# Splitting the first casts, deferring three row picks, and swapping a half quarter with the third convolution

## The chip, the cores and the metric

The kernel runs on one core of a Trainium2 chip. Its engines appear in the profile as PE (TensorE: matrix multiplications, with the weight loads as PEld), DVE (VectorE), ACT (ScalarE), POOL (GpSimd) and SP (SyncE, which here only issues transfers). Each engine takes its instructions in the order of the program and waits where an operand, a buffer or a transfer is not ready. The metric is the device time of one execution in microseconds (us); less is better.

## The reference

For each of 8 batches, 4096 positions and 8 heads the reference makes seven weights by a softmax, and forms a causal convolution of `x` with them (24 channels to a head). The result, 32768 rows of 192 numbers, goes through a feed-forward layer with a squared ReLU:

```python
w = np.exp(weight_gen - max);  w = w / (sum + 1e-09)          # (8, 4096, 8, 7)
out = np.einsum('bshk,bskhg->bshg', w, x_unf)                 # x_unf: 7 shifted rows of x
h = np.maximum(out.reshape(B * S, D) @ w_in, 0.0)             # 192 -> 2048
return h * h @ w_out                                          # 2048 -> 192
```

Inputs and outputs are 32-bit floats.

## The kernel before, in words

The rows are cut into 64 sub-blocks of 512. Blocks 0 and 1 hold one sub-block each, all later ones hold two. For each block there are five kinds of work:

- **Softmax** (class `Softmax`): exponentials on ACT (L238, called "E" in the plans), then sums, reciprocals and products on DVE (L245, L252, L260, called "S"). The weights end in a tile with 8 rows to a partition, `v_first`.
- **Rows and bands.** A band matrix needs the weights with one row to a partition. For the first two sub-blocks PE does this re-ordering: `select_rows` (L359) multiplies with a 0/1 matrix, 8 multiplications for each of five row tiles ("row picks"), and ACT copies each result to `wr` (L377). For later ones, DMAs do it (`wr_load_sbuf`, L351). `st_band` (L381, called "B") then spreads `wr` over a mask on DVE, and gives `bd`.
- **Convolution** ("C"): `bd` against `x` on PE (L447 for the first two sub-blocks, L519 for the next blocks), into PSUM tiles `yp`, which ACT or DVE copies to `y` (L459, L460, L462, L530).
- **Units** ("u"): `st_unit` multiplies `y` with a slice of `w_in` into a PSUM tile `h` (L549 in blocks 0 and 1, where there are 8 units, L564 after, where there are 16). ACT takes the ReLU, `t` (L578), and for each pair of units DVE squares it, `g` (L582).
- **Half quarters** ("M"): `st_mm2` multiplies `g` with `w_out` on PE into the banks o0 and o1 (L613). Every second one ends with `o_sum`: an ACT copy (L627), and from block 2 on a DVE addition (L629), before the store.

PSUM holds o0 and o1 and a ring of three larger tiles, tag "h", which picks, `yp` and `h` share: a unit can start only when the tile of three allocations before has been read.

The order is written out by hand: the program is traced in the order in which each engine is to work. What comes before the first unit is a straight list (L667 to L718). The list `plans` (L725) then has a string for each of blocks 0 to 3; steps "M" take half quarters, block after block, from one generator. In blocks 0 and 1 the four half quarters of a block are those of quarter 0 and 1 over units 0 to 3, then of quarter 0 and 1 over units 4 to 7. So of the four M in `plans[1]` three belong to block 0 and the fourth is the first of block 1.

In the straight list, `x_cast` (L333) casts all five row tiles of the first `x` from 32 to 16 bits in one ACT instruction (L335), before the picks. `st_conv_first` (L431) calls `next_rows` (L702) after each of its five tiles: one row pick of the second sub-block each time, ACT copies for the first two, and after the second the cast of the first half of `w_in` (L708, 1536 columns, on ACT). The copies of the other three rows follow the convolution.

Of the kernel before, what the change touches and what calls it, by code (L numbers as in the profile page):

```python
# [9 lines left out]
def kernel(  # L10
# [26 lines left out]
    nc = tc.nc  # L37
    f32 = mybir.dt.float32
    f16 = mybir.dt.float16

    B, S, D = x.shape
# [9 lines left out]
    P = 128  # L51
# [14 lines left out]
    NT = 5  # L66
# [4 lines left out]
    ROW_ORDER = (0, 1, 2, 3, 4)  # L71
# [9 lines left out]
    p_x = ctx.enter_context(tc.tile_pool(name="p_x", bufs=2))  # L81
# [12 lines left out]
    NQ = Dff // WQ  # L94
    w_i = const.tile([P, WQ, 2, NQ + NQ // 2], f16, name="w_i")
# [32 lines left out]
    x_st = {}  # L128
# [10 lines left out]
    def cross_w_in(q):  # L139
        for r0, r1 in ((0, RT), (RT, 0)):  # L140
            nc.sync.dma_start(out=w_i[r0 : r0 + RT, q, 1], in_=w_i[r1 : r1 + RT, q, 0])
# [147 lines left out]
    x_t, wr_t, pr_t, bd_t, yp_t, y_t, g_t, gp_t, t1_t, o_t, o_sb_t = ({} for _ in range(11))  # L289
# [12 lines left out]
    def tile_start(j, i):  # L302

        t1 = (j % NBB + 1) * TB
        return TB - P if i == NT - 1 and t1 in ends(j // NBB) else starts[i]
# [17 lines left out]
    def x_load(j):  # L323
        x_t[j] = p_x.tile([P, NT, D], f16, name="xt")
        block_load(j, x_t[j], x[j // NBB], D, nc.gpsimd)
# [4 lines left out]
            j, x_st[j][:, 0 : NT * D].rearrange("p (t d) -> p t d", t=NT), x[j // NBB], D, nc.sync  # L330
        )

    def x_cast(j, copy):  # L333
        x_t[j] = p_x.tile([P, NT, D], f16, name="xt")
        copy(out=x_t[j].rearrange("p t d -> p (t d)"), in_=x_st[j][:, 0 : NT * D])  # L335

    def wr_load(j):
        wr_t[j] = p_wr.tile([P, NT, HP, SL * 2], f16, name="wr")
# [20 lines left out]
    def select_rows(j, s, tiles, places):  # L359

        if j not in wr_t:
            wr_t[j] = p_wr.tile([P, NT, HP, SL * 2], f16, name="wr")
        for i, (pool, tag) in zip(tiles, places):
            pr = pool.tile([P, H * SL], f32, name="pr", tag=tag)
            a = max(j % NBB * TB + tile_start(j, i), 0) - s.t0
            for r in range(s.r):
                c = a + FIRST - 1 - r
                nc.tensor.matmul(  # L368
                    out=pr, lhsT=sel[:, c : c + P],
                    rhs=s.v[:, HALO + r].rearrange("p g c e -> p (g c e)"),  # L370
                    start=(r == 0), stop=(r == s.r - 1),
                )
            pr_t[(j, i)] = pr

    def copy_rows(j, tiles):
        for i in tiles:
            nc.scalar.copy(  # L377
                out=wr_t[j][:, i].rearrange("p g c -> p (g c)"), in_=pr_t.pop((j, i))
            )

    def st_band(j, tiles):  # L381


        if j not in bd_t:
            bd_t[j] = p_bd.tile([P, H * NT * STEP], f16, name="bd")
        i = tiles[0]
        lo = STEP * i
        shift = 0 if i == 0 and j % NBB == 0 else lo - tile_start(j, i)
        n = min(STEP, P - shift)
        shape = (P, HP * len(tiles), n // SL, 2 * SL)  # L390
        nc.vector.tensor_tensor(  # L391
            out=bd_t[j][:, H * lo : H * (lo + len(tiles) * n)].rearrange(
                "p (g m c) -> p g m c", g=shape[1], c=2 * SL
            ),
            in0=wr_t[j][:, i : tiles[-1] + 1]
            .rearrange("p t g c -> p (t g) c")
            .unsqueeze(2)
            .broadcast_to(shape),
            in1=mask[:, shift : shift + n]
            .rearrange("p (m c) e -> p m (c e)", c=SL)  # L400
            .unsqueeze(1)
            .broadcast_to(shape),
            op=AluOp.mult,
        )
# [26 lines left out]
    def st_conv_first(j, between=None):  # L431

        s = BLOCKS[j][0]
        y = p_y.tile([P, NK, TB], f16, name="y")
        y_t[j] = y
        yp = ps_h.tile([P, 2, TB], f32, name="yp", tag="h")
        places = [(q, 32 * q, 0) for q in range(4)]
        places += [(q, r0 + 32 * (q - 4), 1) for r0 in (0, RT) for q in (4, 5)]
        for i in ROW_ORDER:
            lo, b = bounds[i], bounds[i + 1]  # L440
            hi = lo + (STEP if tile_start(s, i) == starts[i] else b - lo)
            bd = bd_t[s][:, H * lo : H * hi].rearrange("p (g c e) -> p g e c", g=HP, e=2)
            for later in (True, False):
                for q, p0, k in places:
                    _, ha, hb, pre = quads[q]
                    m, h = (32, hb) if later else (pre, ha)
                    nc.tensor.matmul(  # L447
                        out=yp[p0 : p0 + m, k, lo:b],
                        lhsT=x_t[s][:, i, 32 * q : 32 * q + m],
                        rhs=bd[:, h // 2, h % 2, 0 : b - lo],  # L450
                        start=True,
                        stop=True,
                        skip_group_check=True,
                        tile_position=(0, p0),
                    )
            if between:
                between(i)
        if j == 0:
            nc.scalar.copy(out=y[:, 0], in_=yp[:, 0])  # L459
            nc.vector.tensor_copy(out=y[:, 1], in_=yp[:, 1])  # L460
        else:
            nc.scalar.copy(out=y[:, 0:2], in_=yp)  # L462
# [178 lines left out]
    def st_bands(j):  # L641
        first = int(j % NBB == 0)
        last = NT - int(tile_start(j, NT - 1) != starts[-1])
        for tiles in (range(first), range(first, last), range(last, NT)):
            if tiles:
                st_band(j, tiles)

    with nc.allow_low_precision("fp16 matmul pipeline"), tc.manual_schedule():
# [31 lines left out]
        s0, s1, s2 = parts[:3]  # L680
# [4 lines left out]
        w_st = p_wg.tile([P, (R + HALO) * HK], f32, name="w_st", tag="wg")[:, 0 : NQ + NQ // 2]  # L685
# [6 lines left out]
        s0.total(0, s0.rh)  # L692
        s0.recip(0, s0.rh)
        s0.scale(0, s0.rh, nc.vector)
        x_cast(0, nc.scalar.copy)
        o0, o1, ring = (ps_o, "o0"), (ps_o, "o1"), (ps_h, "h")
        select_rows(0, s0, ROW_ORDER, (o1, ring, ring, ring, o0))
        copy_rows(0, ROW_ORDER)
        for i in ROW_ORDER:
            st_band(0, (i,))  # L700

        def next_rows(i):  # L702
            n = ROW_ORDER.index(i)
            select_rows(1, s0, (i,), ((o1, ring, ring, o0, o1)[n],))
            if n < 2:
                copy_rows(1, (i,))
            if n == 1:
                nc.scalar.copy(out=w_i[:, 0, 0], in_=w_st)  # L708

        st_conv_first(0, next_rows)  # L710
        copy_rows(1, ROW_ORDER[2:])

        nc.gpsimd.tensor_copy(out=gate, in_=w_st[:, 0:1])
        for q in range(4):
# [8 lines left out]
        steady = "MuMuuu" * 3 + "MuuuMCu"  # L723
        steady_spread = "MuMuuu" * 2 + "MuCMuuu" + "MuMuuu"
        plans = {  # L725
            0: "B1 u u u u E1 C S1 u u M u u",
            1: "L3 u u B2 M E2 B3 u M E2 u u S2 S2 u M u C u M",
            2: "L4 u u u E3 M u u u M B4 u u u u M B5 S3 u u u u M u E3 C u",
            3: "L5 L6 S3 u u u M u u u M u M B6 E4 u u u M u M B7 u u u E4 M u M C S4 u",
        }  # L730

# [50 lines left out]
        for j in range(len(plans), NBLK):  # L782
            plan, u = [], 0
# [9 lines left out]
        def load_rows(j):  # L793

            s = [p for p in parts if p.fb <= j][-1]
            if s.r == FIRST:
                return
            if s in stored:
                for n in range(BLOCKS[j][0], sum(BLOCKS[j])):
                    wr_load(n)  # L800
            else:
                waiting.append((s, j))
# [40 lines left out]
        for j in range(NBLK):  # L843
            if j + 2 < NBLK:
                load_rows(j + 2)
            if j == 1:
                for q in range(WQ):
                    cross_w_in(q)
            u = 0
            for step in plans[j].split():  # L850
                kind, n = step[0], int(step[1:] or 0)
                if kind == "u":
                    st_unit(j, u)
                    u += 1
                elif kind == "M":
                    next(mm2)
                elif kind == "C" and j + 1 < NBLK:
                    st_conv(j + 1)
                    if j == 0:
                        x_load(3)  # L860
                    elif j + 2 < NBLK:
                        for k in range(BLOCKS[j + 2][0], sum(BLOCKS[j + 2])):
                            x_load(k)
                    if j == 5:
                        load_w_spread()
                    elif j == 6:
                        cross_w_spread()
                elif kind == "E":
                    parts[n].exp(*next(parts[n].exps))
                elif kind == "S":  # L870
                    soft(parts[n])
                elif kind == "B":
                    st_bands(n)
                elif kind == "L":
                    parts[n].load(nc.sync)


        j = NBLK - 1
# [44 lines left out]
```

The softmax here doesn't subtract the row's maximum and nothing guards it: scores larger than these inputs give would overflow.

## Time and profile before

| what | value |
|---|---|
| runs | 732.98 us, median of 5 (732.74 to 733.24) |
| the profiled execution | 732.74 us, span from first to last instruction 731.0 us |
| PE busy in the span | 724.5 us, 99% |
| DVE busy | 625.8 us, 86% |
| ACT busy | 612.7 us, 84% |
| POOL busy | 99.9 us, 14% |
| granted TensorE clock | 1.00 |

By stage, from the busy time of each engine in stretches of the span (us):

| stretch | what it holds | length | PE | DVE | ACT |
|---|---|---|---|---|---|
| 0 to 13.5 | up to the first unit | 13.5 | 10.84 | 8.26 | 6.70 |
| 13.5 to 22.2 | block 0 | 8.7 | 8.56 | 7.84 | 7.84 |
| 22.2 to 35.7 | block 1 | 13.5 | 13.47 | 12.23 | 12.49 |
| 35.7 to 59.7 | block 2, start of block 3 | 24.0 | 23.67 | 22.50 | 22.63 |
| 59.7 to 731.0 | the rest | 671.3 | 667.91 | 574.98 | 563.08 |

The profile is one execution on the chip. A line of the timeline has start, duration, engine, source line, operation, the tiles written and read, and how often; what stands in brackets is the idle time of the engine just before, and what ended it. A chain of waits is followed back from the last instruction, at each step to what released it. A merged line's duration runs from its first start to its last end. Ends of multiplications are modelled, so the distance between two starts says more of PE than a duration does.

### The profile page before, as it was taken

How to read it: one execution, taken by the hardware profiler on the slowest of the kernel's cores; microseconds unless marked ns; L12 is line 12 of the kernel's file. 1: busy time of each engine (PE TensorE's matmuls, PEld its weight loads, DVE VectorE, ACT ScalarE, POOL GpSimd, SP SyncE). 2: the span in 40 equal slices, each digit the busy share in tenths (PEclk: the TensorE clock that was granted, in tenths of full speed). 3: DMA queues.
4: the chain of work that ended last, by engine and by line, in shares of the span. 5: the costliest groups of instructions: out<-in, count | busy, mean ns of one | idle time of the engine just before them, and what ended most of it. 6: DMA issues, size and time to landing. Idle time of an engine off the chain costs nothing.

```text
span 731.0 us, 30985 instructions
## 1 busy us (share of the span) xinstructions
PE 724.5 (99%) x14053; PEld 529.1 (72%) x14053; DVE 625.8 (86%) x834; ACT 612.7 (84%) x731; POOL 99.9 (14%) x145
## 2 busy tenths in 40 slices
PE   8999999999999999999999999999999999999998
PEld 4658788777777777777777777777777777777777
DVE  6998998998898988888988888988889988778753
ACT  5899888888888888888888888888888888888883
POOL 8231223321001100011000010010000110001000
PEclk9999999999999999999999999999999999999999
DMA  9555445684445452455432554334544325444012
GB/s 205 114 111 109 82 78 112 142 150 121 94 66 137 87 95 56 85 117 119 72 69 63 128 113 87 56 74 119 103 88 86 57 51 119 66 87 78 30 45 68
DMA packets 125984, 68.30 MB, mean 93 GB/s; under 512 B 85321, under 2 KB 122140, under 8 KB 125340
## 3 DMA queue, kind: packets, MB, share of 16 engines
q1 hardware_dynamic: 79516, 46.79, 22.5%
q0 software_dynamic: 46192, 19.43, 22.5%
q8 instruction: 110, 1.80, 1.0%
q14 instruction: 22, 0.18, 0.1%
q10 hardware_dynamic: 144, 0.10, 0.0%
HBM read 50.18 MB, written 28.70 MB: 108 GB/s over the span
## 4 chain that ended last, share of the span: by engine, by line
PE 95%; DVE 3%; ACT 1%; DMA 0%; issue 0%; DVEq 0%
PE o L613 46%; PE h L564 42%; PE yp L485 4%; PE h L549 2%; PE yp L519 1%; DVE g L582 1%; DVE bd L391 1%; DMA wg<-in_weight_gen_dram 0%; DVE v_first L260 0%; ACT t L578 0%; DVE ssum L245 0%; DVE rcp L252 0%; PE yp L447 0%; ACT w_i L708 0%; PE pr L368 0%
## 5 line engine op out<-in xcount | busy, mean ns | idle before, releaser
L578 ACT ACTIVATE t<-h 128x1024 f16<-128x1024 f32 x512 | 496.5, 1027 | 60.7 <-PE h L564 59.2
L613 PEld LDWEIGHTS <-g 64*128 64x128 f16 (+1 forms) x8032 | 344.6, 94 | 55.1 <-issue 2.6
L613 PE MATMUL o<-w_o,g 64*128 64x192 f16 (+1 forms) x8032 | 380.5, 243 | 0.4 <-issue 0.2
L582 DVE TENSOR_TENSOR g<-t 128x2048 f16<-128x2048 f16 (+1 forms) x287 | 307.2, 1104 | 28.4 <-ACT t L578 28.1
L564 PE MATMUL h<-y,w_p 64*128 64x512 f16 x2400 | 291.7, 376 | 0.0
L564 PEld LDWEIGHTS <-w_p 64*128 64x128 f16 x2400 | 113.9, 94 | 94.7
L391 DVE TENSOR_TENSOR bd<-wr,mask 128x4160 f16<-128x4160 f16 (+3 forms) x89 | 149.3, 1702 | 1.4 <-ACT wr L377 0.7
L629 DVE TENSOR_TENSOR o_sb<-o,o_sb 128x384 f32<-128x384 f32 x123 | 68.3, 555 | 62.5 <-ACT o_sb L627 58.7
L321 POOL DMA_DIRECT2D xt<-in_x_dram x63 | 52.6, 839 | 415.5 <-PE yp L485 362.4
L627 ACT COPY o_sb<-o 128x384 f32<-128x384 f32 x129 | 61.6, 477 | 45.7 <-PE o L613 44.5
L564 PE MATMUL h<-y,w_i 64*128 64x512 f16 x576 | 70.8, 376 | 0.1
L564 PEld LDWEIGHTS <-w_i 64*128 64x128 f16 x576 | 31.2, 94 | 21.4 <-issue 1.4
L485 PEld LDWEIGHTS <-xt 128*32 128x32 f16 x2000 | 24.4, 95 | 10.6 <-issue 10.6
L260 DVE TENSOR_TENSOR v_big<-ex,rcp 128x112 f16<-128x112 f32 (+5 forms) x180 | 29.8, 235 | 1.9 <-DMA vd<-v_big 0.9
L495 DVE CAST y<-yp 128x1024 f16<-128x1024 f32 x25 | 30.4, 1216 | 0.0
L485 PE MATMUL yp<-bd,xt 128*32 128x104 f16 (+1 forms) x2000 | 28.3, 209 | 0.0
L238 ACT ACTIVATE ex<-wg 128x560 f32<-128x560 f32 (+4 forms) x38 | 25.9, 683 | 2.0 <-DMA wg<-in_weight_gen_dram 2.0
L245 DVE TENSOR_REDUCE ssum<-ex 128x80 f32<-128x560 f32 (+4 forms) x38 | 25.3, 665 | 1.4 <-ACT ex L238 1.4
L495 ACT CAST y<-yp 128x1024 f16<-128x1024 f32 x25 | 25.2, 1007 | 0.0
L252 DVE RECIPROCAL rcp<-ssum 128x80 f32<-128x80 f32 (+4 forms) x38 | 22.8, 600 | 1.3
L311 POOL DMA_DIRECT2D xt<-in_x_dram x7 | 3.9, 555 | 123.8 <-PE yp L485 109.4
L351 POOL DMA_DIRECT2D wr<-v_first x24 | 12.9, 560 | 22.3 <-ACT t L578 11.7
(40 smaller groups left out, 115.6 us busy)
## 6 DMA issues: line engine op xcount, KB each, us to landing
out_dram<-o_sb SPq DMA_DIRECT2D x63, 384.0 KB
xt<-in_x_dram POOLq DMA_DIRECT2D x42, 240.0 KB, 5.0
wg<-in_weight_gen_dram SPq DMA_DIRECT2D x4, 1064.0 KB
xt<-in_x_dram POOLq DMA_DIRECT2D x21, 192.0 KB, 4.8
wr<-vd SPq DMA_DIRECT2D x38, 80.0 KB
vd<-v_big SPq DMA_DIRECT2D x5, 512.0 KB
y<-y SPq DMA_DIRECT2D x100, 24.0 KB
wg<-in_weight_gen_dram SPq DMA_DIRECT2D x3, 616.0 KB
```

What stands on the lines that cost most here:

```text
L238: nc.scalar.activation(out=self.ex[:, lo:hi].rearrange("p r g k e -> p (r g) k e"), in_=self.wg[:, lo:hi].rearrange("p r (g e) k -> p (r g ...
L260: eng.tensor_tensor(out=bass.AP(tensor=v.tensor, offset=v.offset + lo * H * SL + lo % SL * 2 + g * SL * 2, ap=[list(v.ap[0]), [H * SL + 2, ...
L321: eng.dma_start(out=dst[:, first:last], in_=ap)
L391: nc.vector.tensor_tensor(out=bd_t[j][:, H * lo : H * (lo + len(tiles) * n)].rearrange("p (g m c) -> p g m c", g=shape[1], c=2 * SL), in0= ...
L485: nc.tensor.matmul(out=yp[p0 : p0 + 32, k - k0, a:b], lhsT=x_t[s][:, i, c0 : c0 + 32], rhs=bd[:, head // 2, e, 0 : b - a], start=True, sto ...
L495: copy(out=y[:, k0 : k0 + 2], in_=yp)
L564: nc.tensor.matmul(out=h[:, half], lhsT=w_in_chunk(w, u, slot, half), rhs=y_t[j][r0 : r0 + RT, k], start=(slot == 0), stop=(slot == NK - 1 ...
L578: nc.scalar.activation(out=t1[:, e], in_=h, func=ActF.Relu)
L582: nc.vector.tensor_tensor(out=g[:, a : e + 1], in0=t1[:, a : e + 1], in1=t1[:, a : e + 1], op=AluOp.mult)
L613: nc.tensor.matmul(out=oo[:, cc * Dm : (cc + 1) * Dm], lhsT=g[r0 : r0 + n, cc * P : (cc + 1) * P], rhs=w_o[r0 : r0 + n, fc, :], start=(fc ...
L627: nc.scalar.copy(out=o_sb, in_=o[0][:, c])
L629: nc.vector.tensor_tensor(out=o_sb, in0=o[1][:, c], in1=o_sb, op=AluOp.add)
```

## The change

Four things are re-arranged; no arithmetic is added or left out.

- The cast of the first `x` is made in three pieces on ACT: row tile 0, tiles 1 and 2, and, behind the ACT copies of the first two picked rows, tiles 3 and 4.
- The cast of the first half of `w_in` is halved: columns 0 to 767 on ACT, 768 to 1535 on DVE.
- Of the five row picks of the second sub-block, the first two stay inside the first convolution. Those of rows 2 and 3 and their copies follow it. That of row 4 and its copy is a new step "P" in `plans[0]`, after the first unit; the bands of the second sub-block ("B1") now stand behind it.
- In `plans[1]` the fourth M moves from the end to a place ahead of C, the third convolution. In `plans[2]` the first M moves from behind three units to the very start, and the units are spread differently between the four M: 0, 5, 4 and 5 units stand ahead of them in the place of 3, 3, 4 and 4.

```diff
-    def x_cast(j, copy):
-        x_t[j] = p_x.tile([P, NT, D], f16, name="xt")
-        copy(out=x_t[j].rearrange("p t d -> p (t d)"), in_=x_st[j][:, 0 : NT * D])
+    def x_cast(j, copy, lo, hi):
+        if j not in x_t:
+            x_t[j] = p_x.tile([P, NT, D], f16, name="xt")
+        copy(
+            out=x_t[j][:, lo:hi].rearrange("p t d -> p (t d)"),
+            in_=x_st[j][:, lo * D : hi * D],
+        )
...
-        x_cast(0, nc.scalar.copy)
+        x_cast(0, nc.scalar.copy, 0, 1)
+        x_cast(0, nc.scalar.copy, 1, 3)
         o0, o1, ring = (ps_o, "o0"), (ps_o, "o1"), (ps_h, "h")
         select_rows(0, s0, ROW_ORDER, (o1, ring, ring, ring, o0))
-        copy_rows(0, ROW_ORDER)
+        copy_rows(0, ROW_ORDER[:2])
+        x_cast(0, nc.scalar.copy, 3, NT)
+        copy_rows(0, ROW_ORDER[2:])
         for i in ROW_ORDER:
             st_band(0, (i,))
 
         def next_rows(i):
             n = ROW_ORDER.index(i)
-            select_rows(1, s0, (i,), ((o1, ring, ring, o0, o1)[n],))
             if n < 2:
+                select_rows(1, s0, (i,), ((o1, ring)[n],))
                 copy_rows(1, (i,))
             if n == 1:
-                nc.scalar.copy(out=w_i[:, 0, 0], in_=w_st)
+                c = (NQ + NQ // 2) // 2
+                nc.scalar.copy(out=w_i[:, 0, 0, 0:c], in_=w_st[:, 0:c])
+                nc.vector.tensor_copy(out=w_i[:, 0, 0, c:], in_=w_st[:, c:])
 
         st_conv_first(0, next_rows)
-        copy_rows(1, ROW_ORDER[2:])
+        select_rows(1, s0, ROW_ORDER[2:4], (ring, o0))
+        copy_rows(1, ROW_ORDER[2:4])
...
-            0: "B1 u u u u E1 C S1 u u M u u",
-            1: "L3 u u B2 M E2 B3 u M E2 u u S2 S2 u M u C u M",
-            2: "L4 u u u E3 M u u u M B4 u u u u M B5 S3 u u u u M u E3 C u",
+            0: "u P B1 u u u E1 C S1 u u M u u",
+            1: "L3 u u B2 M E2 B3 u M E2 u u S2 S2 u M u M C u",
+            2: "L4 M u u u u E3 u M B4 u u u u M B5 S3 u u u u u M u E3 C u",
...
+                elif kind == "P":
+                    select_rows(1, s0, ROW_ORDER[4:], (o1,))
+                    copy_rows(1, ROW_ORDER[4:])
```

## The prediction

> **What bounds the kernel now.** I read the page first: which engine carries the chain, and where it is anything else.
>
> ```profile
> PE 724.5 (99%) x14053; PEld 529.1 (72%) x14053; DVE 625.8 (86%) x834; ACT 612.7 (84%) x731; POOL 99.9 (14%) x145
> PE 95%; DVE 3%; ACT 1%; DMA 0%; issue 0%; DVEq 0%
> ```
>
> PE is the bound. Its work is only re-ordered here, so the time can change only by PE's waits, and by the stretches show these lie before 59.7 us; after that PE is busy for 667.9 of 671.3 us. So I ask one thing: how much earlier or later does PE reach the place that it now reaches at 59.68? Five answers of the timeline carry this. ACT ahead of the first unit:
>
> ```profile
> 7.56 0.99 ACT L335 CAST xt<-x_st 128x960 f16<-128x960 f32 x1 [2.54 <-DMA x_st<-in_x_dram]
> ...
> 11.39 1.48 ACT L708 CAST w_i<-w_st 128x1536 f16<-128x1536 f32 x1
> 12.87 0.58 ACT L459 CAST y<-yp 128x512 f16<-128x512 f32 x1
> ```
>
> The cast of w_in ends at 12.87, and the copy of y starts in that moment. The x cast ends at 8.55, before the first picked row (8.84): it costs nothing now. What follows the copy, all engines:
>
> ```profile
> 13.49 0.69 DVE L460 CAST y<-yp 128x512 f16<-128x512 f32 x1 [1.74 <-ACT y L459]
> 13.51 0.38 PE L549 MATMUL h<-y,w_i 128*128 128x512 f16 x1 [0.34 <-ACT y L459]
> ```
>
> PE, then DVE, around the third convolution:
>
> ```profile
> 31.77 1.82 PE L519 MATMUL yp<-bd,xt 128*32 128x104 f16 x120
> 33.52 0.93 PE L549 MATMUL h<-y,w_i 64*128 64x512 f16 x4
> 34.28 1.48 PE L613 MATMUL o<-w_o,g 128*128 128x192 f16 x16
> 35.70 0.60 PE L564 MATMUL h<-y,w_i 64*128 64x512 f16 x4
> ```
>
> ```profile
> 27.57 4.59 DVE L391 TENSOR_TENSOR bd<-wr,mask 128x4160 f16<-128x4160 f16 x3 [0.65 <-DMA wr<-v_first]
> 32.08 1.22 DVE L582 TENSOR_TENSOR g<-t 128x2048 f16<-128x2048 f16 x1
> ```
>
> The half quarter at 34.28 is block 1's first, over units 0 to 3. Its second half needs the g of units 2 and 3, which stands behind the bands and ends at 33.30. ACT in block 2, and PE at the end of the stretch:
>
> ```profile
> 36.56 2.85 ACT L578 ACTIVATE t<-h 128x1024 f16<-128x1024 f32 x3 [0.96 <-PE h L564]
> ...
> 52.46 0.51 ACT L238 ACTIVATE ex<-wg 128x336 f32<-128x336 f32 x1
> 52.87 1.49 ACT L530 CAST y<-yp 128x1024 f16<-128x1024 f32 x2
> ```
>
> ```profile
> 59.25 0.24 PE L613 MATMUL o<-w_o,g 64*128 64x192 f16 x1
> 59.68 1.00 PE L613 MATMUL o<-w_o,g 64*128 64x192 f16 x20 [0.19 <-DVE o_sb L629]
> ```
>
> Between 36.56 and 52.87 ACT idles only 0.12, 0.25 and 0.14 us: it has next to no slack in block 2.
>
> **What the Trainium skill says.** "ScalarE: Activation LUTs", section "What ACT_TABLE_LOAD costs": an instruction with immediate operands takes 186 ns plus 0.833 ns per element. The trace agrees: 960 columns took 992 ns (986), 1536 took 1476 ns (1466). "VectorE: DVE Perf Modes", "The perf-mode tier table": a copy of 2048 fp32 elements from SBUF takes 1227 ns at 2x. No row here shows such a copy. "TensorEngine Tiling (Array Packing)", "Key Properties": changing the tiling mode drains TensorE. The trace agrees: a convolution row with a pick behind it took 0.64 us (9.89 to 10.54), though a row alone takes 0.21 (80 multiplications in 1.05 us, 16.81 to 17.86) and eight pick multiplications 0.23 (8 x 29 ns). "PSUM — Partial Sum Buffer", "PSUM bank collisions raise a hardware error": engines on different banks don't collide. Still DVE's copy of y waits for ACT's half in another bank of the tile (13.45, then 13.49), so I let it wait in the new order too.
>
> **The change part by part.** Sums are made in the profiled execution (732.74 us, span 731.0, 1.74 around it); the runs' median is 0.24 above it, and I move the result by as much.
>
> *Casts.* ACT's half of w_in: 186 + 0.833 x 768 = 0.83 us, 11.39 to 12.22, where the whole took 1.48. Now the convolution decides. Without picks between its last three rows, its fifth row waits for the fifth band: bands start every 0.50 us from 9.16, the fifth ends at 11.75, PE follows 0.15 later (9.75 to 9.89 for the first) and needs 0.36. So yp is ready at 12.26 and the copy of y starts at 12.31 and not 12.87: **0.56 earlier**. DVE's half follows the fifth band (from 11.67). By the page's figure for 2048, with the excess over 1024/0.96 ns kept, 768 columns at 2x are (768/2)/0.96 + 160 = 0.56 us; at 1x, 0.96. I take 2x; at either it ends before 12.93, where DVE's copy of y can start, so ACT's y copy hides it. Behind 12.93 it would be paid in full. The x pieces: tiles 3 and 4 cost 186 + 0.833 x 384 = 0.51 us of ACT between the second and third copies, 9.28 to 9.79. The third copy ends near 10.00, and the third band, paced by DVE, starts at 10.17: hidden by some 0.06 us after the handover of 0.11; beyond that all later bands move.
>
> *Picks.* Rows 2 and 3 run on PE from 12.2 to 12.8, while PE waits for y until 12.94: hidden, with 0.1 to spare. Their copies (0.1 us apiece in sequence) fall into ACT's wait before the first t (0.86 idle). Row 4 stands between units 0 and 1, where PE has no wait: 0.64 - 0.21 = **0.43 us** with its mode changes (0.23 if these cost nothing). Its ACT copy comes behind the first t, about 0.1 to 0.2 us; t of unit 1 then comes about 0.3 earlier than now. B1 waits for the copy, but its main band (four tiles) needs only rows 0 to 3 and runs 13.5 to 15.4; behind B1 on DVE is the first g, due at 16.2. Sum so far at unit 1 on PE: 0.56 - 0.43 = **0.13 us ahead**.
>
> *Transfers.* No DMA is added. S1 moves 0.3 ahead, and with it the row transfers of B2, which SP and POOL issue in the old order. The one that the band waited for landed at 27.55, after its other packets (26.33), behind PE's own instruction fetch of 25.5 to 26.5. That moves with PE, so I let the bands move by 0.13 (0.30 if the fetch did not matter). SP's and POOL's other issues (x, w_out, the crossing of w_in) keep their place in their queues, and wait for nothing new that is late.
>
> *M ahead of the third convolution.* PE arrives at 31.77 - 0.13 = 31.64. The half quarter takes 1.32 (29.60 to 30.92): 0.66 for units 0 and 1 to 32.30. Then it needs g: 33.30 - 0.13 + 0.05 = 33.22, **a wait of 0.92**; behind it on PE is the convolution, whose bands are ready by then. Half quarter done 33.88; convolution 1.53 (51.43 to 52.96, without its wait; now 1.75, so **0.22 saved**) to 35.41; unit 7 0.76 to 36.17. Then the moved first M of `plans[2]`, 1.42 (34.28 to 35.70), to 37.59. Block 2's unit 0 starts there and not at 35.70: 1.42 of moved work, and 0.47 net loss.
>
> *ACT in block 2.* Its first t comes 0.86 after unit 0: 38.45, and was 36.56. From there to the first y copy of the fourth convolution ACT has 16.31 - 0.51 idle = 15.80 us of work, none of it removed. So that copy comes at 54.25 at the earliest, and not 52.87: **1.38 late**. PE alone would be only 0.47 late, but a unit's h needs the t of three units before, so PE waits, most behind the runs of five units. Unit 0 of block 3 waits for that copy (53.92 now), so 55.30.
>
> *The end of the stretch.* Now PE loses 59.68 - 59.25 - 0.06 = 0.37 us to DVE's addition. Its chain starts from g's that also come late; I get the addition's end at about 60.6 with the 1.38 on PE, so the wait is gone. **1.38 - 0.37 = 1.0 us later.** Profiled execution 733.75, median **734.0 us**, +0.14%. With the open bounds (pick 0.23, bands 0.30 ahead, ACT idling 0 to 0.5 as now, 0.2 of the last wait left) 733.4 to 734.7.
>
> **Rivals.** Differences within 0.2% (1.47 us) can't be told from no change.
> 1. *Ahead after all.* The g of units 2 and 3 is ready when the moved M needs it, and ACT keeps up: -0.13 - 0.22 - 0.37 = -0.72, 732.3 us; with the fifth pick free too, 731.8. For: each of those waits is in the trace. Against: g is behind 4.5 us of bands, which the transfer and not PE sets off.
> 2. *Slower beyond 0.2%: a ring tile.* If the pick of row 2 is given the tile of yp, it waits for DVE's copy of y (13.62), and unit 0, behind it on PE, starts at 13.66 + 0.57 for two picks = 14.2 in place of 12.94. 1.0 + 1.3 = +2.3, 735.3 us. It decides once it adds 0.47. Against: the tile of an earlier pick has been free since 9.7.
> 3. *The start gains nothing.* If the x piece pushes the bands by 0.5 us, y is copied no earlier: 1.0 + 0.56, 734.5 us.
>
> **Numbers.** Forecast 0.56 (0.09 of it above 1.47 us), first rival 0.22, second 0.12, third 0.10, of which about half exceeds 1.47 us. For a gain beyond 0.2% no sum above suffices; I leave 0.05 of the first rival for what I don't see. Faster 0.05; slower 0.09 + 0.12 + 0.06 = 0.27; within 0.68. The range goes to the ends of the first two rivals, 732.3 to 735.3; the forecast's own is 733.4 to 734.7.
>
> **What would show it.** Right: y's ACT copy at 12.3, the first unit at 12.9, a wait of about 0.9 inside the fourth M of `plans[1]`, block 2's first t near 38.4, ACT without idle until the y copy near 54.2. Wrong: a third band after 10.2; that M without a wait; PE in block 2 without waits for t; or a wait after 60 us, of which I expect none.

## The result, and the profile after

| kernel | median | lowest to highest | runs |
|---|---|---|---|
| before | 732.97 us | 732.17 to 733.77 | 50 |
| after | 734.62 us | 733.22 to 735.66 | 30 |

The ratio is 1.0021, with a 95% interval of 1.0016 to 1.0026: 1.65 us slower, just across the 0.2% (1.47 us) that stood for no change, and with an interval that reaches to both sides of it. The profiled execution took 734.86 us, span 733.2 (before 732.74 and 731.0), at a granted clock of 1.00. The chain is still PE's, with more waits in it (93% in place of 95%):

```profile
PE 725.0 (99%) x14053; PEld 528.6 (72%) x14053; DVE 626.6 (85%) x835; ACT 611.9 (83%) x733; POOL 100.2 (14%) x145
PE 93%; DVE 2%; ACT 1%; issue 1%; DMA 0%; DVEq 0%; ACTq 0%
```

One thing must be taken off first. In this execution the very first transfer landed later: the first exponential on ACT starts at 4.34 us and not at 4.09 (3.96 to 4.13 in all other kernels here), and the picks and bands of the first sub-block are 0.24 late with it. Nothing ahead of it was changed, so below "net" means less 0.25. In the code after, the lines from L340 to L690 of before have moved down by 4.

ACT ahead of the first unit, from the timeline:

```profile
9.42 0.52 ACT L336 CAST xt<-x_st 128x384 f16<-128x384 f32 x1
...
11.64 0.84 ACT L716 CAST w_i<-w_st 128x768 f16<-128x768 f32 x1
12.46 0.59 ACT L463 CAST y<-yp 128x512 f16<-128x512 f32 x1
```

The copy of y starts 0.41 earlier than before (12.87), net 0.66. DVE's share of it, and PE from the convolution on:

```profile
11.92 0.55 DVE L717 CAST w_i<-w_st 128x768 f16<-128x768 f32 x1
13.08 0.69 DVE L464 CAST y<-yp 128x512 f16<-128x512 f32 x1 [0.61 <-ACT y L463]
```

```profile
12.35 0.64 PE L372 MATMUL pr<-v_first,sel 128*128 128x64 f16 x16
13.10 1.12 PE L553 MATMUL h<-y,w_i 128*128 128x512 f16 x4
14.15 0.41 PE L372 MATMUL pr<-v_first,sel 128*128 128x64 f16 x8
14.49 2.44 PE L553 MATMUL h<-y,w_i 64*128 64x512 f16 x12
```

Unit 0 starts at 13.10, not 13.51; unit 1 at 14.49, with the pick of row 4 between them. PE around the third convolution, and DVE there:

```profile
31.79 0.83 PE L617 MATMUL o<-w_o,g 128*128 128x192 f16 x8
33.75 0.83 PE L617 MATMUL o<-w_o,g 128*128 128x192 f16 x8 [1.12 <-DVE g L586]
34.51 1.60 PE L523 MATMUL yp<-bd,xt 128*32 128x104 f16 x120
36.05 0.93 PE L553 MATMUL h<-y,w_i 64*128 64x512 f16 x4
36.81 1.48 PE L617 MATMUL o<-w_o,g 128*128 128x192 f16 x16
38.23 2.76 PE L568 MATMUL h<-y,w_i 64*128 64x512 f16 x24
```

```profile
27.96 4.59 DVE L395 TENSOR_TENSOR bd<-wr,mask 128x4160 f16<-128x4160 f16 x3 [1.16 <-DMA wr<-v_first]
32.47 1.22 DVE L586 TENSOR_TENSOR g<-t 128x2048 f16<-128x2048 f16 x1
```

The fourth half quarter of block 1's plan now falls into two: 8 multiplications, then a wait for the g that ends at 33.69. The two lines at 36.05 and 36.81 are unit 7 and the M that was moved to the head of block 2. ACT in block 2:

```profile
39.09 3.77 ACT L582 ACTIVATE t<-h 128x1024 f16<-128x1024 f32 x4 [0.99 <-PE h L568]
...
48.67 4.69 ACT L582 ACTIVATE t<-h 128x1024 f16<-128x1024 f32 x5
54.14 1.02 ACT L582 ACTIVATE t<-h 128x1024 f16<-128x1024 f32 x1 [0.79 <-DVE g L586]
55.06 0.51 ACT L238 ACTIVATE ex<-wg 128x336 f32<-128x336 f32 x1
55.47 1.00 ACT L534 CAST y<-yp 128x1024 f16<-128x1024 f32 x1
```

Here is a wait that the kernel before did not have: 0.79 us ahead of the t of unit 14, for DVE. There the bands B5, then S3 and only then the g of units 8 and 9 (the first of the four in the last line, done near 54.1) follow each other:

```profile
48.58 2.35 DVE L395 TENSOR_TENSOR bd<-wr,mask 128x3328 f16<-128x3328 f16 x2
...
52.09 0.83 DVE L260 TENSOR_TENSOR v_first<-ex,rcp 128x112 f16<-128x112 f32 x4
52.84 4.09 DVE L586 TENSOR_TENSOR g<-t 128x2048 f16<-128x2048 f16 x4
```

And PE at the end of the stretch:

```profile
56.52 2.24 PE L568 MATMUL h<-y,w_i 64*128 64x512 f16 x18 [0.48 <-ACT y L534]
...
61.84 1.54 PE L617 MATMUL o<-w_o,g 64*128 64x192 f16 x32
```

The half quarter that waited for DVE's addition (59.25, then 59.68) now runs in one piece, but 2.16 later. From there to the end of the span both executions take the same (671.32 us before, 671.36 after), so what was lost was lost ahead of it.

### The profile page after: what moved, and what is told of

Read it like the earlier page. It is cut to its first block, busy times and chain, and to the rows that moved or that the text cites. A ratio compares the mean times of both kernels' runs of the same rounds, so it can differ in the third digit from the quotient of the medians.

```text
span 733.2 us, 30986 instructions
## 1 busy us (share of the span) xinstructions
PE 725.0 (99%) x14053; PEld 528.6 (72%) x14053; DVE 626.6 (85%) x835; ACT 611.9 (83%) x733; POOL 100.2 (14%) x145
## 4 chain that ended last, share of the span: by engine, by line
PE 93%; DVE 2%; ACT 1%; issue 1%; DMA 0%; DVEq 0%; ACTq 0%
PE o L617 45%; PE h L568 43%; PE yp L489 4%; PE yp L523 1%; DVE bd L395 1%; ACT t L582 1%; DVE g L586 0%; DMA wr<-v_first 0%; ACT y L534 0%; PE h L553 0%; DVE v_first L260 0%; DVE rcp L252 0%; DVE ssum L245 0%; ACT ex L238 0%; ACT o_sb L631 0%
```

## The experiments

Every kernel was timed beside the kernel before on the same chip; "of before" is that kernel's median in the same session. There were three sessions (733.23, 733.22 and 733.40), so kernels of different sessions are compared by their ratios.

| kernel | median, us | of before, us | ratio | 95% interval |
|---|---|---|---|---|
| start only | 732.80 | 733.23 | 0.9995 | 0.9987 to 1.0003 |
| plans only | 735.07 | 733.23 | 1.0027 | 1.0016 to 1.0037 |
| M ahead of the third convolution, with the start | 733.71 | 733.23 | 1.0006 | 0.9998 to 1.0014 |
| four buffers for pairs of t | 734.25 | 733.23 | 1.0012 | 1.0006 to 1.0019 |
| B3 later | 732.75 | 733.22 | 0.9994 | 0.9986 to 1.0002 |
| S3 later | 734.05 | 733.22 | 1.0009 | 1.0003 to 1.0016 |
| three picks behind the convolution | 732.95 | 733.22 | 0.9995 | 0.9987 to 1.0004 |
| block 2's plan only, with the start | 734.07 | 733.22 | 1.0010 | 1.0003 to 1.0017 |
| three picks, and unit 7 first | 732.17 | 733.40 | 0.9983 | 0.9977 to 0.9990 |
| unit 7 first, the start as before | 732.79 | 733.40 | 0.9991 | 0.9983 to 0.9999 |
| start only, w_in cast whole | 733.50 | 733.40 | 1.0002 | 0.9993 to 1.0010 |

My theory (A) was that the start is a small gain and the moved half quarters are the whole loss. The rivals: the loss is in the start (B), or in block 2's plan alone (C).

**Start or plans.** First the changed start with the plans of blocks 1 and 2 as before:

```diff
-            1: "L3 u u B2 M E2 B3 u M E2 u u S2 S2 u M u M C u",
-            2: "L4 M u u u u E3 u M B4 u u u u M B5 S3 u u u u u M u E3 C u",
+            1: "L3 u u B2 M E2 B3 u M E2 u u S2 S2 u M u C u M",
+            2: "L4 u u u E3 M u u u M B4 u u u u M B5 S3 u u u u M u E3 C u",
```

> The start of the changed kernel (cast pieces, three picks behind the convolution, P between units 0 and 1) with the plans of blocks 1 and 2 as before. Theory A (the loss is all in the moved half quarters): the start is ahead by 0.1 to 0.3 us at unit 1 and stays so; against the kernel before -0.1 to -0.6 us. Theory B (the loss is in the start: the pick among the units, and rows of the bands B2 that land later): about +1 to +1.6 us, the whole loss. First copy of y near 12.2 to 12.5 in the trace under both.

Then the reverse, the kernel before with these two plans as changed:

> The start as before, only the plans of blocks 1 and 2 changed. Theory A: the fourth M of block 1's plan waits about 0.9 to 1.3 us for the g of units 2 and 3, block 2's unit 0 starts 0.5 to 0.9 us later than the 1.42 us of the moved M alone, ACT is about 1.5 to 2 us late at the copy of y of the fourth convolution; in all +1.5 to +2.2 us against the kernel before. Theory B: within 0.4 us of it.

The start alone comes out 0.4 us faster with an interval that includes no change; the plans alone are 2.0 us slower (1.2 to 2.7). So B falls. The start is no loss beyond 0.2 us, and the plans account for all of it.

**Which of the two plans.** With block 1's plan as changed and block 2's as before:

```diff
-            2: "L4 M u u u u E3 u M B4 u u u u M B5 S3 u u u u u M u E3 C u",
+            2: "L4 u u u E3 M u u u M B4 u u u u M B5 S3 u u u u M u E3 C u",
```

> The changed kernel with the plan of block 2 as before: only the M ahead of the third convolution is left of the moves. Theory A in its first form (the wait for g is the loss): the wait of 0.9 to 1.3 us is still there, less the 0.22 us that the convolution saves and the 0.37 us of the wait for DVE's addition; with the start's gain in it 0 to +0.6 us against the kernel before. Theory C (the loss comes from block 2's plan, whose M stands ahead of its first unit and keeps ACT idle for 1.4 us): -0.2 to +0.2 us. Theory B: the whole +1.6 us.

And with block 2's as changed and block 1's as before:

```diff
-            1: "L3 u u B2 M E2 B3 u M E2 u u S2 S2 u M u M C u",
+            1: "L3 u u B2 M E2 B3 u M E2 u u S2 S2 u M u C u M",
```

> The changed kernel with the plan of block 1 as before, so that two half quarters in a row stand ahead of block 2's first unit. No M waits for g of units 2 and 3. If ACT's lack of slack in block 2 is the second term of the loss: ACT starts block 2 about 1.4 us later than in the kernel before and never gets it back, of which 0.2 to 0.4 are covered by the vanishing wait for DVE's addition; with the start's gain +0.5 to +1.2 us against the kernel before. If only the M's wait counts: -0.2 to -0.5 us.

The first is 0.4 us slower than before, with an interval that includes no change, the second 0.7 (0.2 to 1.2). Measured from the start alone (0.4 us faster), block 1's move costs 0.8 us and block 2's 1.1 us; together 1.9, where the changed kernel stands 1.9 above the start alone (1.0021 less 0.9995). The two add up, which speaks against my first form of A, in which M's wait for g is the whole loss, and against C alone. The intervals of single terms are some 0.6 us to either side, so the times alone leave the split open; the sum is firmer. The trace of the first kernel shows M's wait again: 1.28 us.

**What block 2's plan costs.** ACT's wait for the g of units 8 and 9 was the new thing in the trace. The pairs of t have three buffers, so the t of unit 14 needs that g done, and in the changed plan the g stands behind B5 and S3 on DVE: ten units stood ahead of B5 before, and nine do now, so unit 9, the second of its pair, comes behind it. Two kernels take that away in different ways. One gives the pairs a fourth buffer:

```diff
-    p_t1 = ctx.enter_context(tc.tile_pool(name="p_t1", bufs=3))
+    p_t1 = ctx.enter_context(tc.tile_pool(name="p_t1", bufs=4))
```

> The changed kernel with four buffers in place of three for the pairs of t. The wait of ACT (0.79 us) ahead of t of unit 14 of block 2, for the g of units 8 and 9 behind B5 and S3 on DVE, must go. If this wait is a term of the loss: 0.4 to 0.8 us faster than the changed kernel, that is +0.8 to +1.2 us against the kernel before. If ACT's lateness comes from block 2's late start alone and the wait only takes the place of another one: as the changed kernel, +1.4 to +1.7 us.

The other leaves the buffers and moves S3 behind that g:

```diff
-            2: "L4 M u u u u E3 u M B4 u u u u M B5 S3 u u u u u M u E3 C u",
+            2: "L4 M u u u u E3 u M B4 u u u u M B5 u u S3 u u u M u E3 C u",
```

> The changed kernel, three buffers of t pairs as in it, with S3 of block 2's plan two units later, behind the g of units 8 and 9. If ACT's wait of 0.79 us for that g is a term of the loss: -0.4 to -0.8 us against the changed kernel, that is +0.8 to +1.2 against the kernel before. If S3 then only holds the next g up and ACT waits there: as the changed kernel, +1.4 to +1.7.

They are 0.9 and 0.7 us slower than before: 0.7 and 0.9 us better than the changed kernel. ACT in the kernel with four buffers:

```profile
38.46 3.77 ACT L582 ACTIVATE t<-h 128x1024 f16<-128x1024 f32 x4 [0.97 <-PE h L568]
...
48.05 5.84 ACT L582 ACTIVATE t<-h 128x1024 f16<-128x1024 f32 x6
53.78 0.51 ACT L238 ACTIVATE ex<-wg 128x336 f32<-128x336 f32 x1
54.19 1.49 ACT L534 CAST y<-yp 128x1024 f16<-128x1024 f32 x2
```

No wait is left ahead of the sixth t of the last run, and from the first t to the copy of y it is 15.73 us; with S3 later 15.72 (38.71 to 54.43); in the changed kernel 16.38 (39.09 to 55.47). Two independent ways of removing one wait give the same gain, so this wait is shown to be a term of the loss, of 0.7 to 0.9 us by the medians (each interval touches that of the changed kernel) and 0.65 by the traces. The rest of block 2's 1.1 us was not taken apart. With block 2's plan only, ACT stands idle for 2.30 us ahead of its first t there, and for 0.96 in the kernel before; that fits what the prediction says of ACT's lack of slack.

**What block 1's move costs.** If M merely waits for a g that stands behind all the bands, the g can be put between them:

```diff
-            1: "L3 u u B2 M E2 B3 u M E2 u u S2 S2 u M u M C u",
+            1: "L3 u u B2 M E2 u M E2 u B3 u S2 S2 u M u M C u",
```

with block 2's plan as before.

> As the kernel with only the M ahead of the third convolution (block 2's plan as before), but in block 1's plan B3 stands behind the fourth unit: DVE makes the g of units 2 and 3 between the bands of B2 and those of B3, near 30.2 to 31.4 us. If the loss of that kernel is the M's wait for this g behind all bands: the wait of 1.1 us is gone, the convolution still saves its 0.22, its last band is ready near 33.7 and its use comes later; -0.8 to -1.2 us against the kernel with only the M moved, so -0.2 to -0.7 against the kernel before. If the wait turns into one of the convolution for the later bands, or block 2 is bound by ACT anyway: 0 to +0.5 us against the kernel before.

It is 0.9 us faster than the kernel with M moved alone (0.9994 against 1.0006; the intervals just overlap), and the wait is gone from its trace: so the wait was the loss. But it is no faster than the start alone. PE there:

```profile
31.42 1.49 PE L617 MATMUL o<-w_o,g 128*128 128x192 f16 x16
32.85 1.98 PE L523 MATMUL yp<-bd,xt 128*32 128x104 f16 x120
```

M runs through, and the convolution now takes 1.91 us to the next start (34.76) in place of 1.54: part of the wait has gone into it. From the rows' landing on, DVE has 4.6 us of bands, and a g of 1.2 set between them delays the bands behind it.

**Where the start's gain goes.** The pick between units 0 and 1 costs PE 0.45 us. So I put all three behind the first convolution, with the plans as before:

```diff
-        select_rows(1, s0, ROW_ORDER[2:4], (ring, o0))
-        copy_rows(1, ROW_ORDER[2:4])
+        select_rows(1, s0, ROW_ORDER[2:], (ring, o0, o1))
+        copy_rows(1, ROW_ORDER[2:])
...
-            0: "u P B1 u u u E1 C S1 u u M u u",
+            0: "B1 u u u u E1 C S1 u u M u u",
```

> The changed start, but all three late picks behind the first convolution and none among the units; the plans as before. The pick among the units cost PE about 0.43 us (it starts unit 1 that much later). Behind the convolution PE waits for y, about 0.6 us of which two picks take; the third is expected to put the first unit 0.05 to 0.25 us later. So 0.2 to 0.4 us better than the start with P: -0.6 to -0.8 us against the kernel before. If the third pick costs as much there: no better than the start with P, -0.2 to -0.5.

The third pick costs nothing there: unit 0 starts 4.01 us after the first ACT copy of picked rows with it (8.77 to 12.78) and without it (8.84 to 12.85). PE comes to the third convolution at 31.05 and not at 31.55. Yet the time is the same as with P (0.9995 both). PE in this kernel:

```profile
31.05 0.23 PE L523 MATMUL yp<-bd,xt 128*32 128x104 f16 x2
31.60 1.88 PE L523 MATMUL yp<-bd,xt 128*32 128x104 f16 x118 [0.33 <-DVE bd L395]
33.42 0.93 PE L553 MATMUL h<-y,w_i 64*128 64x512 f16 x4
```

The convolution took 2.37 us where its work is 1.54. It waits for bands, and DVE waits for the rows of B2: 1.22 us of idle time ahead of 27.42, only 0.15 earlier than before, though S1 ended 0.72 earlier (22.23 against 22.95). So a new theory (D): beyond some 0.2 us, what the start gains is lost there. If so, work that needs nothing of DVE should fill the wait. Unit 7 is such work, and it was right behind the convolution:

```diff
-            1: "L3 u u B2 M E2 B3 u M E2 u u S2 S2 u M u C u M",
+            1: "L3 u u B2 M E2 B3 u M E2 u u S2 S2 u M u u C M",
```

> The start with all three late picks behind the first convolution, block 2's plan as before, and in block 1's plan unit 7 in place of a half quarter ahead of the third convolution (unit 7 needs nothing of DVE; its M stays behind the convolution). Theory D: what the start gains (PE is 0.6 to 0.7 us ahead at 31 us) is lost in the third convolution, which waits for bands whose rows land no earlier. Then unit 7 (0.76 us) fills that wait, the convolution ends where it ended without it, and block 2 starts 0.6 to 0.8 us earlier: -0.8 to -1.2 us against the kernel before. If the gain is lost elsewhere, or unit 7 delays the copies of y on ACT as much: as without it, -0.1 to -0.4 us.

> The kernel before, start and all, with only unit 7 moved ahead of the third convolution. Under theory D there is just the 0.22 us of the convolution's wait to fill: -0.1 to -0.4 us against the kernel before. If filling is worth 0.6 us or more by itself (so that the start has no part in it): -0.6 to -1.0 us.

With the three picks it is 1.2 us faster than the kernel before (0.7 to 1.7), where three picks alone gave 0.4 (the two intervals overlap); with the start of before 0.7 us (0.1 to 1.2), more than D allowed. PE in the first of them:

```profile
30.30 1.67 PE L553 MATMUL h<-y,w_i 128*128 128x512 f16 x8
31.90 1.60 PE L523 MATMUL yp<-bd,xt 128*32 128x104 f16 x120
33.43 1.49 PE L617 MATMUL o<-w_o,g 128*128 128x192 f16 x16
34.86 2.12 PE L568 MATMUL h<-y,w_i 64*128 64x512 f16 x18
```

Units 6 and 7 run on end, the convolution takes its bare 1.53 us and ends at 33.43, as it did with the wait (33.42). Block 2 begins at 34.86, 0.84 earlier than before and 0.74 earlier than with three picks alone (35.60). In this trace, then, the start's gain is no longer lost at the convolution, as D says. Of the 0.84 us some 0.3 is given back: the wait for DVE's addition near 59 us grows, and that half quarter goes on at 59.16, 0.52 earlier than before. This kernel beats both.

The times don't settle D. With the start of before, unit 7 first was worth 0.7 us. D allowed 0.1 to 0.4; 0.6 and more I had written down for the case that the start has no part in it. That 0.7 and the start's 0.4, simply added, are 1.1, close to the 1.2 measured. Nor does the trace of that kernel show 0.7: its block 2 begins 0.26 earlier (35.44), its half quarter near 59 us goes on 0.17 earlier (59.51). The profiled execution of the kernel before (732.74) was itself 0.5 to 0.7 us faster than that kernel's medians in these sessions. So its wait in the convolution, 0.21, may be smaller than usual and the filling of it worth more; no run here shows whether it is.

**The halved cast by itself.** The start alone, with w_in cast whole on ACT:

```diff
-                nc.scalar.copy(out=w_i[:, 0, 0, 0:c], in_=w_st[:, 0:c])
-                nc.vector.tensor_copy(out=w_i[:, 0, 0, c:], in_=w_st[:, c:])
+                nc.scalar.copy(out=w_i[:, 0, 0], in_=w_st)
```

> The changed start with the plans of before, but the first half of w_in cast whole on ACT as before. By the prediction's step the copy of y then comes 0.6 us later, and unit 0 too, so that unit 1 is about 0.4 us behind the kernel before (the pick among the units is still there). Under theory D the bands of B2 follow S1, which is later now: 0 to +0.5 us against the kernel before, 0.3 to 0.7 more than the start with the halved cast.

Unit 0 starts at 13.39, 0.54 later than with the halved cast (12.85), and the time is 0.1 us above before, 0.5 above the start alone. The size in the trace is firm; that it reaches the end is not shown, since the intervals (0.9993 to 1.0010, and 0.9987 to 1.0003) overlap.

## Why the prediction was right or wrong

The likeliest case, a small loss by M's wait and by ACT's lack of slack, was the right one; the forecast of 734.0 was 0.6 us too low. The median lies 0.1 us inside the forecast's own range, and the profiled execution (734.86) just outside it; the 1.65 us are also just beyond the 1.47 that I gave 0.68 to stay within. So the mechanism was right, but that the range held is in part luck: two terms were too small, by 0.39 and 0.58 us, and nothing made up for them. By steps, in the profiled executions:

| step | predicted | measured |
|---|---|---|
| copy of y | 0.56 earlier | 0.66 net |
| DVE's half of w_in | 0.56 us, hidden | 0.55, hidden |
| pick of row 4 between units | 0.43 | 0.45 (unit 0 to 1: 1.39, before 0.94) |
| PE at unit 1 | 0.13 ahead | 0.21 net |
| bands of B2 | 0.13 earlier | 0.14 later, net |
| wait in the moved M | 0.92 | 1.30 (31.79 + 0.66 to 33.75) |
| convolution's wait saved | 0.22 | 0.21 (1.75 to 1.54) |
| block 2's unit 0, without the moved M | 0.47 late | 0.86 net (38.23 - 35.70 - 1.42 - 0.25) |
| ACT, first t to copy of y | 15.80 | 16.38 |
| end of the stretch | 1.0 late | 1.91 net (61.84 - 59.68 - 0.25) |

*Casts and picks* were right to a tenth. DVE's copy of 768 columns confirms the price taken from the Trainium skill ("VectorE: DVE Perf Modes", "The perf-mode tier table"): 0.55 us is the 2x tier, which an estimate from that page's figure puts at 0.56, and 1x at 0.96. Seven of the eight other kernels with this copy have 0.55 too; in one (block 2's plan only) it took 0.80, for a reason that no run shows. The x piece did not move the bands: they start 0.24 us later than before throughout, which is the late first transfer. The two deferred picks hid, and the third rival (the start gains nothing) was wrong of the trace. It was half right of the time: the start alone is worth about 0.4 us, with an interval that includes nothing; if more of it is lost, then by the trace at the third convolution's wait for bands, which the rival did not name.

*Transfers*: this step failed in the profiled execution. I let the bands of B2 follow PE. S1's last product did end 0.13 earlier (22.82 against 22.95; net 0.38), but the rows took longer to land: 5.1 us from there to the first band, where the kernel before took 4.6. The size of M's wait follows: g later by 0.27 net than I had it, PE earlier by 0.10, together nearly the 0.38 by which the wait was too small. That the change delays the rows is not shown. Five other kernels do the same work in the same order up to these bands, and theirs start at 26.82 to 27.74; with the start only it is 27.29, 0.28 earlier than before, as I had it for the case that the fetch doesn't matter (0.30). In the four other kernels that move M and leave the bands where they are, M's wait is 0.86 to 1.28 us, so the predicted 0.92 is within what occurs.

*ACT in block 2*: the claim was "ACT without idle until the y copy". ACT's work is indeed 15.7 to 15.8 us, as the two kernels without the wait show, but I never asked whether t has a free buffer. B5 and S3 stand ahead of the g of units 8 and 9 on DVE, and five units follow them without a pause: when ACT came to unit 14, the pair three back, units 8 and 9, was still unread. That is the missed wait of 0.79, of which 0.58 shows between the two ends.

*The end*: right. The wait for DVE's addition is gone, and the timeline shows no wait of PE behind 63 us; from block 3's unit 0 (2.60 later) to that half quarter (2.16 later) 0.44 came back, predicted 0.37.

Together: 1.0 + 0.39 (block 2's start) + 0.58 - 0.07 = 1.90, the measured net 1.91. The medians differ by less, 1.65; one profiled execution of each kernel does not show how much of this is the landing of rows in that execution.

Of the rivals, the first (ahead) failed at its condition, the g that should be ready. The second, a pick that waits for a ring tile, did not occur: the two picks ran at 12.35 to 12.99 and unit 0 followed at once.

## What to carry to other kernels

Before moving work ahead of a wait, look at what else the moved work itself waits for: here a half quarter that needs DVE's g could not fill a wait caused by DVE, while a unit that needed nothing of DVE's late work could. A gain ahead of a stage that waits for transfers may be lost in that stage; look for it behind the stage and not only where it is made. And when units are regrouped between other work, check for each buffer ring how many of its readers now stand behind long instructions, not just how busy the writer is.

## What the runs showed of the hardware that I had not expected

The 16 KB row transfers of B2 are the same in all these kernels, issued by SP and POOL in each, and still the time from the end of S1's last product to the first band was 4.6 us in the kernel before, 4.7 to 4.9 in four others, 5.1 to 5.2 in the changed kernel and six more, and in one (block 2's plan only) the rows were there within 3.9 us (22.94 to 26.82), with no wait at all. Among the six kernels that do the same work in the same order up to there, the changed one included, it is 3.9 to 5.1 us. One 16 KB instruction fetch of PE lies in that stretch in each; it took 1.03 us before and 1.37 us after, and 1.02 to 1.18 us in the four with 4.7 to 4.9. But two kernels with a fetch of 0.88 us had 5.2, so that the fetch delays the rows is not shown; no kernel was made to test it, and the cause stays open. These differences of up to 1.3 us between single executions are as large as most effects measured here.
